# Sixteen 32x32 tiles for the query side, one stock of PSUM, and both FFN weights cast by their transfers

## The chip, the cores and the metric

The kernel runs on one core of a Trainium2 chip. Its engines are TensorE (PE; its weight loads are listed apart as PEld), VectorE (DVE), ScalarE (ACT), GpSimd (POOL) and SyncE (SP). Each works through its own instructions in their order and waits at semaphores for the others. Matmuls write only to PSUM, which has 8 banks of 512 fp32 per partition. Data come from and go to the main memory by DMA; a transfer is issued by SP, ACT or POOL, and one issued by POOL can change the type on the way.

The metric is the device time of one execution in microseconds (us). A profile shows one execution; its span goes from the first to the last instruction.

## The reference

Four batches, four heads, 1088 positions, head size 32. Keys and queries go through two sketches of size 8, and the product of the two gives 64 features; linear attention follows, and a feed-forward layer with SiLU on all 4352 tokens of 128 values:

```python
def phi(x):                                     # S1, S2: 8 x 32
    a = einsum('rd,bhsd->bhsr', S1, x)
    b = einsum('rd,bhsd->bhsr', S2, x)
    return einsum('bhsi,bhsj->bhsij', a, b).reshape(..., 64)
q_p, k_p = phi(q), phi(k)
kv  = einsum('bhsf,bhsd->bhfd', k_p, v)
z   = sum(k_p, axis=2)
num = einsum('bhsf,bhfd->bhsd', q_p, kv)
den = einsum('bhsf,bhf->bhs', q_p, z)[..., None] + 1e-06
x   = (num / den).transpose(0, 2, 1, 3).reshape(4352, 128)
h   = x @ w_in                                  # 128 x 2048
out = (h * sigmoid(h)) @ w_out                  # 2048 x 128
```

All inputs and the output are fp32.

## The kernel before

**Layout.** Positions are split as 32 rows of 34 (`NY`): K and Q of a batch are loaded so that a partition is a head (4) times one of 32 rows, and 34 positions of 32 values lie along it. DVE transposes blocks of 32x32, so after `kt` or `qt` a partition is a head times a value. w_in is 128 x 2048, cut in 16 (`NJ`) blocks of 128 columns.

**Order.** Nothing is scheduled by a planner at build time: the text `ORDER` lists the steps, each line of it is executed from left to right, and so each engine's program has its instructions in this order. A step that waits holds up everything behind it on its engine.

**Keys of a batch b.** `kt` transposes K (DVE), `pk` makes the sketches by matmuls in fp32 on tiles of 64 rows x 32 columns of the array, `tk` transposes them back, four `kp` multiply the two sketches (bf16), `kv` sums keys times values in 18 matmuls; `zs`, `zc`, `mm` and `mk` make the sum z and put it as third weight beside the query sketches in `WQ` (L308). `kw` or, for batch 0, `kw_act` masks KV and puts it in `KVw` with a second copy in the other half of the partitions.

**Queries.** `qt` transposes Q; `pq` (L346) makes both sketches and the denominator's weights by fp32 matmuls on four 64x64 tiles: two groups `g` of positions times two pairs `r` of heads; `tq` transposes back; `dn` is four DVE operations on the denominator; `qo` makes the 64 features (bf16); `pt` transposes them; `nm` (L388) multiplies by KV, again on four 64x64 tiles; `xc` copies the result to `xT`, the FFN's input, in bf16. Each batch goes through this in two parts (positions 0 to 8 and 8 to 17 of 17 pairs), batch 0 in three.

**FFN.** Tokens are cut in ten chunks (`CHUNKS`). For each, `f1` (L415) multiplies xT by two blocks of w_in (four for chunks of at most 256 tokens), `sl` is the SiLU on ACT (L428), `f2` (L431) adds up the products with w_out in one bank `o_ps`, with w_out as weights and g as moving data. `ot` (L442) transposes o_ps on DVE to rows of 32 and stores them with four transfers on SP in pieces of 128 bytes, eight where the chunk crosses a batch.

**PSUM.** `psH`: two pairs of banks for h (and for some calls of batch 0 marked H); `psP`: one pair for pk, pq and nm; `psO`: one bank for o_ps and the zero matmuls; `psA`: one bank for z, m and kv.

**Loads.** S1 and S2 come by ACT's queue, four times repeated over `T16`, and DVE transposes them (`weights`, L234). w_in is loaded in fp32 by SP in four parts, and ACT casts it with `wic` (L458), which also permutes the columns so that a block is contiguous. w_out is cast by its transfer, which POOL issues in `wo` (L250). `zeros` (L228) are matmuls on zeros between the first steps.

Of the kernel before, what the change touches and what calls it, by code (L numbers as in the profile page):

```python
# [26 lines left out]
f2 0 0, f1 0 3, sl 0 2, f2 0 1, pt 0 4 10, kt 1 0 34
sl 0 3, nm 0 4 10 H, f2 0 2, xc 0 4 10 A, f2 0 3, dn 0 10 17
f1 1 0, sl 1 0, ot 0, f1 1 3, sl 1 3, pk 1
qo 0 10 17, f1 1 1, tk 1, f1 1 6, kt 2 0 34, f2 1 0  # L30
sl 1 1, qt 1 0 34, lv 1, lv 2, f1 1 7, f2 1 1
sl 1 6, pt 0 10 17, f1 1 2, sl 1 7, sl 1 2, zs 1
pk 2, f1 1 5, zc 1 A, mm 1, tk 2, f1 1 4
sl 1 5, sl 1 4, f2 1 2, f2 1 3, nm 0 10 17 H, xc 0 10 17 A
mk 1, zs 2, kp 1 1 0, pq 1 0 8, kp 1 0 0, f1 2 3
f1 2 1, kp 1 0 1, f2 1 4, zc 2 A, f2 1 5, f2 1 6
sl 2 3, sl 2 1, f1 2 0, f2 1 7, sl 2 0, f1 2 5
tq 1 0 8, kp 1 1 1, sl 2 5, kv 1, f1 2 2, sl 2 2
dn 1 0 8, ot 1, f2 2 0, f1 2 4, sl 2 4, qo 1 0 8
kw 1, f2 2 1, f1 2 6, sl 2 6, f2 2 2, pt 1 0 8  # L40
kt 3 0 34, pq 1 8 17, nm 1 0 8 H, f1 2 7, f2 2 3, xc 1 0 8 A
sl 2 7, f2 2 4, f1 3 0, sl 3 0, tq 1 8 17, pk 3
f1 3 1, f2 2 5, lv 3, sl 3 1, dn 1 8 17, qo 1 8 17
pt 1 8 17, f1 3 5, mm 2, f2 2 6, tk 3, f1 3 7
mk 2, sl 3 5, sl 3 7, f2 2 7, f1 3 2, ot 2
nm 1 8 17, f1 3 3, f2 3 0, sl 3 2, f2 3 1, qt 2 0 34
sl 3 3, xc 1 8 17 V, f1 3 6, kp 2 1 1, f2 3 2, sl 3 6
f1 4 2, kp 2 0 0, pq 2 0 8, f1 4 3, tq 2 0 8, kp 2 1 0
sl 4 2, f2 3 3, sl 4 3, f1 3 4, pq 2 8 17, kp 2 0 1
sl 3 4, f1 4 7, sl 4 7, dn 2 0 8, kv 2, tq 2 8 17  # L50
f1 4 1, sl 4 1, f2 3 4, qo 2 0 8, kw 2, f1 4 0
f2 3 5, sl 4 0, f2 3 6, pt 2 0 8, f2 3 7, ot 3
f1 4 6, f1 4 4, nm 2 0 8, zs 3, f2 4 0, sl 4 6
sl 4 4, xc 2 0 8 V, dn 2 8 17, qt 3 0 34, f1 4 5, f2 4 1
f1 5 1, f2 4 2, qo 2 8 17, sl 4 5, zc 3 V, sl 5 1
f2 4 3, f1 5 0, sl 5 0, f2 4 4, kp 3 1 1, f1 5 5
f2 4 5, f2 4 6, f1 5 4, sl 5 5, sl 5 4, f2 4 7
pt 2 8 17, f1 5 7, mm 3, nm 2 8 17, kp 3 1 0, f1 5 3
sl 5 7, ot 4, mk 3, f2 5 0, f1 5 2, xc 2 8 17 V
sl 5 3, sl 5 2, pq 3 0 8, f1 5 6, sl 5 6, f2 5 1  # L60
tq 3 0 8, f1 6 1, sl 6 1, pq 3 8 17, f1 6 4, kp 3 0 0
f2 5 2, dn 3 0 8, sl 6 4, f1 6 2, f2 5 3, tq 3 8 17
qo 3 0 8, kp 3 0 1, f2 5 4, f1 6 0, sl 6 2, f2 5 5
f1 6 7, pt 3 0 8, kv 3, dn 3 8 17, sl 6 0, kw 3
sl 6 7, f1 6 5, f2 5 6, f2 5 7, f1 6 6, sl 6 5
nm 3 0 8, f1 6 3, ot 5, xc 3 0 8 V, sl 6 6, f2 6 0
f2 6 1, f1 7 4, sl 6 3, sl 7 4, f2 6 2, f1 7 5
f2 6 3, f2 6 4, sl 7 5, f1 7 1, f2 6 5, qo 3 8 17
f1 7 6, f2 6 6, sl 7 1, f1 7 0, f2 6 7, sl 7 6
sl 7 0, f1 7 2, pt 3 8 17, sl 7 2, nm 3 8 17, f1 7 3  # L70
ot 6, f2 7 0, f1 7 7, f2 7 1, xc 3 8 17 V, sl 7 3
sl 7 7, f1 8 1, f2 7 2, f1 8 5, f2 7 3, sl 8 1
f2 7 4, f1 8 2, f2 7 5, sl 8 5, f1 8 0, f2 7 6
f2 7 7, sl 8 2, f1 8 4, sl 8 0, f1 8 3, ot 7
# [15 lines left out]
def kernel(  # L90
# [22 lines left out]
    NH = NY // 2  # L113
# [94 lines left out]
    for i in range(2):  # L208
        nc.gpsimd.memset(KT[i][:, S:], 0.0)
# [300 lines left out]
```

## Time and profile before

Median of three runs 104.25 us (103.95 to 105.39).

| | us |
|---|---|
| profiled execution | 105.12 |
| its span | 103.1 |
| TensorE busy (864 matmuls) | 89.6 |
| ACT busy | 75.8 |
| DVE busy | 67.7 |
| POOL busy | 12.1 |
| mean granted TensorE clock | 0.949 |

Read the busy times as shares of stages: DVE works mostly in the first two thirds, TensorE and ACT from about 18 us to 97 us. Matmuls are pipelined, and the busy time of one contains its latency: a matmul of 128x512 shows as 379 ns, while two of them take 0.43 us in the chain. In the lists "x16" is the number of instructions; an fp32 matmul counts as two.

### The profile page before, as it was taken

The page shows a single profiled execution, that of the slowest core. Times are in us where ns is not written, and L with a number is a line of the kernel's source. Part 1 is how long each engine was busy: PE and PEld are TensorE (multiplying, and loading weights), DVE is VectorE, ACT ScalarE, POOL GpSimd, SP SyncE. Part 2 cuts the span into 40 slices and gives each one's busy share as a digit, 9 for nine tenths or more (in the row PEclk, how much of TensorE's full clock was granted, in tenths as well). Part 3 has the DMA queues.
Part 4 walks back from the last instruction along what each step waited for, and adds up shares of the span by engine and source line. Part 5 has one row for each costly group of instructions (what it writes and reads, how often), then busy time and mean ns, then how long its engine had stood idle before and what let it go on. Part 6 is the DMA issues. An engine that isn't in the chain of part 4 may idle for free.

```text
span 103.1 us, 2192 instructions
## 1 busy us (share of the span) xinstructions
PE 89.6 (87%) x864; PEld 47.1 (46%) x864; DVE 67.7 (66%) x130; ACT 75.8 (73%) x91; POOL 12.1 (12%) x48
## 2 busy tenths in 40 slices
PE   5719988909999999999999999999999999999700
PEld 5602876506535564443344444434544344456500
DVE  0072999794489999999999999689994230201200
ACT  0506619945297699799999779998988999997500
POOL 5608950002620000000000000000000000000000
PEclk9995999997699999999999999999999999999985
DMA  1898999999690004000400041140003141032331
GB/s 40 281 237 270 304 382 323 331 345 221 87 130 8 0 3 76 7 0 8 85 0 0 6 69 33 31 71 0 6 15 65 22 78 24 0 57 45 69 58 23
DMA packets 23214, 9.82 MB, mean 95 GB/s; under 512 B 19236, under 2 KB 21540, under 8 KB 23204
## 3 DMA queue, kind: packets, MB, share of 16 engines
q1 hardware_dynamic: 20768, 8.29, 30.5%
q0 software_dynamic: 2256, 1.36, 9.3%
q8 instruction: 7, 0.11, 0.5%
q10 hardware_dynamic: 180, 0.02, 0.1%
q14 instruction: 3, 0.02, 0.1%
HBM read 8.80 MB, written 2.23 MB: 107 GB/s over the span
## 4 chain that ended last, share of the span: by engine, by line
PE 63%; DMA 16%; DVE 9%; ACT 1%; POOL 1%; ACTq 1%; issue 1%; DVEq 0%; POOLq 0%
PE o_ps L439 28%; PE h_ps L421 25%; DMA w_out_bf<-in_moe_w_out_dram 13%; DMA T<-in_S_dram 3%; PE pq_ps L354 3%; PE num_ps L395 2%; ACT g L428 1%; DVE PQ L360 1%; DVE kp L286 1%; PE z_ps L295 1%; PE pk_ps L273 1%; DVE KT L260 1%; ACTq L178 1%; DVE o_tt L445 1%; DVE qp L380 1%; PE kv_ps L318 1%
## 5 line engine op out<-in xcount | busy, mean ns | idle before, releaser
L428 ACT ACTIVATE g<-h_ps 128x1024 bf16<-128x1024 f32 (+2 forms) x72 | 65.6, 979 | 10.6 <-PE h_ps L421 10.1
L439 PE MATMUL o_ps<-g,w_out_bf 128*128 128x512 bf16 (+4 forms) x160 | 38.7, 355 | 2.8 <-DMA w_out_bf<-in_moe_w_out_dram 2.6
L421 PE MATMUL h_ps<-xT,w_in_bf 128*128 128x512 bf16 (+4 forms) x160 | 40.8, 351 | 0.1
L439 PEld LDWEIGHTS <-w_out_bf 128*128 128x128 bf16 x160 | 15.5, 100 | 17.3 <-DMA w_out_bf<-in_moe_w_out_dram 2.9
L421 PEld LDWEIGHTS <-w_in_bf 128*128 128x128 bf16 x160 | 14.3, 99 | 16.9 <-issue 7.0
L445 DVE STREAM_TRANSPOSE o_tt<-o_ps 128x512 f32<-128x512 f32 (+4 forms) x10 | 6.3, 634 | 18.7 <-PE o_ps L439 18.6
L286 DVE TENSOR_TENSOR kp<-pk 128x576 bf16<-128x576 f32 x16 | 11.4, 740 | 0.0
L232 PE MATMUL zps<-zw 128*128 128x128 bf16 x112 | 9.6, 249 | 1.1 <-POOL hm L199 1.1
L380 DVE TENSOR_TENSOR qp<-PQ 128x1024 bf16<-128x1024 f32 (+4 forms) x9 | 10.3, 1142 | 0.1
L232 PEld LDWEIGHTS <-zw 128*128 128x128 bf16 x112 | 8.1, 115 | 3.5 <-issue 2.3
L158 POOL DMA_DIRECT2D Vb<-in_v_dram x12 | 6.5, 546 | 11.8 <-DMA w_out_bf<-in_moe_w_out_dram 9.1
L360 DVE STREAM_TRANSPOSE PQ<-pq_ps 128x512 f32<-128x512 f32 (+3 forms) x8 | 5.7, 714 | 1.7 <-PE pq_ps L354 1.6
L386 DVE STREAM_TRANSPOSE qT<-qp 128x512 f32<-128x512 f32 (+4 forms) x9 | 6.0, 671 | 0.2
L354 PE MATMUL pq_ps<-QT,WQ 64*64 64x256 f32 (+3 forms) x64 | 5.3, 401 | 0.1
L343 DVE STREAM_TRANSPOSE QT<-Qx 128x1088 f32<-128x1088 f32 (+2 forms) x5 | 5.3, 1056 | 0.0
L260 DVE STREAM_TRANSPOSE KT<-Kx 128x1088 f32<-128x1088 f32 (+2 forms) x5 | 5.2, 1049 | 0.0
L273 PE MATMUL h_ps<-KT,WK 64*32 64x288 f32 x16 | 2.4, 683 | 3.0 <-DVE KT L260 3.0
L236 DVE STREAM_TRANSPOSE ST<-T 32x32 f32<-32x32 f32 x4 | 0.8, 202 | 5.6 <-DMA T<-in_S_dram 5.6
L226 ACT ACTIVATE w_in_bf<-w_in_f 128x512 bf16<-128x512 f32 x4 | 4.3, 1122 | 0.1
L226 ACT ACTIVATE Vb<-Vx 128x576 bf16<-128x576 f32 x2 | 1.3, 674 | 3.7 <-DMA Vx<-in_v_dram 3.7
L218 ACT ACT_TABLE_LOAD x1 | 1.3, 1283 | 3.4 <-issue 3.4
L337 ACT ACTIVATE KVw<-kv_ps,hm 64x64 bf16<-64x64 f32 (+1 forms) x6 | 1.5, 306 | 3.0 <-PE kv_ps L318 3.0
(53 smaller groups left out, 52.5 us busy)
## 6 DMA issues: line engine op xcount, KB each, us to landing
Kx<-in_k_dram SPq DMA_DIRECT2D x3, 544.0 KB, 10.4
Qx<-in_q_dram SPq DMA_DIRECT2D x3, 544.0 KB, 14.8
w_in_f<-in_moe_w_in_dram SPq DMA_DIRECT2D x4, 256.0 KB, 4.8
out_dram<-o_tt SPq DMA_DIRECT2D x16, 64.0 KB, 1.9
Vb<-in_v_dram POOLq DMA_DIRECT2D x9, 72.0 KB, 14.6
w_out_bf<-in_moe_w_out_dram POOLq DMA_DIRECT2D x1, 512.0 KB, 13.5
out_dram<-o_tt SPq DMA_DIRECT2D x8, 56.0 KB, 1.8
Vx<-in_v_dram SPq DMA_DIRECT2D x3, 144.0 KB, 4.1
```

Source lines behind the costliest of these rows:

```text
L158: ins = eng.dma_start(dst, src)
L232: nc.tensor.matmul(t["zps"][:, :ncol], zw, zw[:, :ncol], start=True, stop=True)
L260: nc.vector.transpose(out=KT[b % 2][:, y0 * 32: y1 * 32], in_=Kx[b][:, y0:y1, :].rearrange("p a d -> p (a d)"))
L286: eng.tensor_tensor(out=o, in0=bcast(s[:, :, 0, 4 * e: 4 * e + 4], 2, R), in1=bcast(s[:, :, 1], 3, 4), op=ALU.mult)
L354: nc.tensor.matmul(t["pq_ps", b, p0][64 * g: 64 * (g + 1), r, :cols].rearrange("p (y x) -> p y x", x=32), w[rs, :], qv[rs, g, p0:p1, :], s ...
L360: nc.vector.transpose(out=PQ[b % 2][:, p0:p1].rearrange("p y r f -> p r y f"), in_=t["pq_ps", b, p0][:, :, :cols].rearrange("p r (y f) -> ...
L380: nc.vector.tensor_tensor(out=t["qp", b][:, p0:p1].rearrange("p y r j i -> p (y r) j i"), in0=bcast(fa, 2, R), in1=bcast(fb, 3, R), op=ALU ...
L386: nc.vector.transpose(out=dst.rearrange("p r (y x) -> p y r x", x=32), in_=src)
L421: nc.tensor.matmul(h[:, i, :], w_in_bf[:, j * P: (j + 1) * P], xT[:, t0: t0 + ntok], start=True, stop=True)
L428: nc.scalar.activation(out=gv, in_=t.pop(("h", c, s)), func=ACT.Silu)
L439: nc.tensor.matmul(op[c][:, :ntok], w_out_bf[:, j, :], g[:, i, :], start=(j == 0), stop=(j == NJ - 1))
L445: nc.vector.transpose(out=o_tt[:, :ntok], in_=op[c][:, :ntok])
```

## The change

**Query side.** A batch (batch 0: three parts) is one call. `pq` and `nm` work on sixteen tiles of 32x32: head `i` by group `c` of four positions, each row of tiles into a bank of its own, so that a call takes two pairs of banks. Blocks of positions are now quadruples, nine for 34 (`NQ`), and QT is padded. `tq` and `xc` come in two calls, one for each pair; `dn`, `qo` and `pt` handle the whole call.

**KV.** `km` masks KV by heads into (2, head, value) in bf16, on DVE, or on ACT in four activations; `kr` multiplies it by the 0/1 matrix `same`, which copies each 32-row strip to all four; `kw` copies the result to `KVw`.

**PSUM.** One stock `psX` of three pairs of banks. Each step names its pair (0, 1, 2) in ORDER: f1, pk, pq and nm share it. `psO` and `psA` stay.

**Weights.** w_in is cast by a transfer that POOL issues in `wi`, after the first part of K has landed; `wo` follows at once. K of batch 1 waits for w_in, Q of batch 1 for w_out. `wic` is gone, and f1 reads its weights with a step of four columns. S1 and S2 are loaded once, by SP and ACT, turned by four matmuls with a unit matrix (`turned`), and masked by one DVE operation.

**Last 768 tokens.** Their order within xT is another. In chunks 8 and 9, f2 takes g as weights and w_out as moving data, 128 columns at a time, so that o_ps holds tokens by row; `ot` copies it and stores it in pieces of 1 KB, two transfers for chunk 8 and one for chunk 9. Chunk 9's o_ps is a pair of the stock. The chunks' bounds from 3136 on are others.

**Order.** ORDER is written anew as a whole; its first lines and a middle part stand below.

```diff
-CHUNKS = [..., (3136, 512), (3648, 512), (4160, 192)]
+CHUNKS = [..., (3136, 448), (3584, 512), (4096, 256)]
+ROWS = 3584
 ORDER = """
-weights, vc0 0 2, kt 0 0 18, kt 0 18 34, zeros 33, pk 0 0 2 H
-weights2, zeros 3, pk 0 2 4, qt 0 0 8, tk 0, zeros 13
...
+wi, wo, zeros 14, turned, weights, kt 0 0 18
+weights2, kt 0 18 27, zeros 14, pk 0 0 0 2, kt 0 27 34, pk 0 -1 2 3
+wq_const, qt 0 0 8, zeros 1, pk 0 -1 3 4, tk 0, kp 0 0 0
+zeros 13, zs 0, zc 0 A, kp 0 1 0, zeros 8, mm 0
+vc0 0 2 A, mk 0 A, kp 0 0 1, vc0 2 4 A, kp 0 1 1, zeros 8
+pq 0 0 2 1 2, zeros 3, kv 0, tq 0 0 2 0, tq 0 0 2 1, dn 0 0 2
+same_const, km 0 A, qo 0 0 2, qt 0 8 34, zeros 18, kr 0
+pt 0 0 2, kw 0 V, zeros 10, pq 0 2 9 0 1, tq 0 2 9 0, zeros 11
+nm 0 0 2 2 0, xc 0 0 2 0 A, tq 0 2 9 1, dn 0 2 5, xc 0 0 2 1 A, zeros 12
+f1 0 0 1, qo 0 2 5, sl 0 0, pt 0 2 5, f1 0 1 2, zeros 12
+nm 0 2 5 0 1, kt 1 0 34, f2 0 0, sl 0 1, xc 0 2 5 1 A, xc 0 2 5 0 A
+dn 0 5 9, f1 0 3 2, qt 1 0 34, f1 0 2 1, sl 0 3, sl 0 2
+pk 1 0, qo 0 5 9, f1 1 3 2, f2 0 1, lv 1, sl 1 3
...
+f1 4 1 2, sl 4 1, f2 3 4, f1 4 0 1, f1 4 4 0, f2 3 5
+qo 2 0 9, kv 2, km 2 V, f1 4 2 2, sl 4 0, f1 4 6 1
+pt 2 0 9, sl 4 4, sl 4 2, kr 2, f1 4 3 0, f2 3 6
+f2 3 7, kw 2 V, sl 4 6, mm 3, ot 3, sl 4 3
+nm 2 0 9 2 1, xc 2 0 9 0 V, mk 3 V, xc 2 0 9 1 V, f2 4 0, f1 4 7 0
...
+f2 8 6, sl 9 1, f2 9 0 1, f2 8 7, sl 9 3, f2 9 1
+ot 8 V, f2 9 2, f2 9 3, ot 9 V
 """
...
+    def bank2(slot, name):
+        return psX.tile([P, 2, CH], FP32, name=f"{name}{slot}", tag=f"x{slot}")
...
+    def turned():
+        t["st"] = psA.tile([P, 2 * R], FP32, name="st_ps", tag="ac")
+        for i in range(4):
+            nc.tensor.matmul(t["st"][32 * i: 32 * (i + 1), :], T16, I16, start=True, stop=True,
+                             tile_position=(0, 32 * i))
...
+    def wi():
+        t["wi"] = begin(nc.gpsimd, w_in_bf, moe_w_in, k0a)
+        load_kq(nc.sync, 1, k, Kx, after=t["wi"])
+    def wo():
+        ins = begin(nc.gpsimd, w_out_bf.rearrange("p (i e) m -> p i (e m)", e=4), ...)
+        load_kq(nc.sync, 1, q, Qx, after=ins)
+        for b in range(2, B):
+            load_kq(nc.sync, b, k, Kx)
+            load_kq(nc.sync, b, q, Qx)
...
+    def kr(b):
+        t["kr", b] = psA.tile([P, 2, H, D], FP32, name="kr_ps", tag="ac")
+        nc.tensor.matmul(..., same, t["km", b].rearrange("p e h d -> p (e h d)"), ...)
+    def kw(b, copy):
+        copy(KVw[b], t["kr", b])
...
+    def pq(b, q0, q1, s0, s1):
+        t["pq", b, q0] = ps = [bank2(s0, "pq_ps"), bank2(s1, "pq_ps")]
+        for c in range(4):
+            for i in range(H):
+                rs = slice(32 * i, 32 * (i + 1))
+                nc.tensor.matmul(ps[i // 2][32 * c: 32 * (c + 1), i % 2, :cols]..., WQ[rs, b, i % 2, :],
+                                 qv[rs, c, q0:q1, :], ..., tile_position=(32 * i, 32 * c))
...
+    def nm(b, q0, q1, s0, s1):
+        t["nm", b, q0] = ps = [bank2(s0, "num_ps"), bank2(s1, "num_ps")]
+        for e in range(2):
+            for i in range(H):
+                for c in range(4):
+                    cs = slice(32 * c, 32 * (c + 1))
+                    nc.tensor.matmul(ps[c // 2][32 * i: 32 * (i + 1), c % 2, :cols],
+                                     KVw[b][cs, e, i, :], t["qT", b][cs, i, q0 * 32: q1 * 32, e],
+                                     ..., tile_position=(32 * c, 32 * i))
...
-            nc.tensor.matmul(h[:, i, :], w_in_bf[:, j * P: (j + 1) * P],
+            nc.tensor.matmul(h[:, i, :], w_in_bf[:, CH * (j // 4) + j % 4: CH * (j // 4 + 1): 4],
                              xT[:, t0: t0 + ntok], start=True, stop=True)
...
+            if t0 >= ROWS:                              # f2
+                if j == 0 and not two:
+                    nc.tensor.matmul(op[c][:, :ntok], zw, bcast(zw, 1, n), start=True, stop=False)
+                for h in range(n):
+                    nc.tensor.matmul(op[c][:, h * P: (h + 1) * P],
+                                     g[:, i, h * P: (h + 1) * P], w_out_bf[:, j, :], ...)
...
+        if t0 >= ROWS:                                  # ot
+            copy(o_tt[:, :ntok], op[c][:, :ntok])
+            for i in range(ntok // (2 * P)):
+                nc.sync.dma_start(dst, o_tt[:, 2 * P * i: 2 * P * (i + 1)])   # pieces of 1 KB
+            return
```

In ORDER, `pq b q0 q1 s0 s1` and `nm` name the two pairs they take, `f1 c s slot` and `pk b slot` one; A and V say whether ACT or DVE copies. The engine's order on DVE after the first slice is qt of the rest, pt, kw, tq; before it was pt, qt, xc.

381 lines of the change are left out of this document (186 added, 195 removed).

## Prediction

> **What bounds the kernel now.** I read in this order: the busy table in stretches over the whole span, which splits it into a start (0 to about 28 us), a middle in which TensorE hardly rests, and an end after 97.4; then the chain that ended last (o_ps and h_ps matmuls 53%, the transfer of w_out 13%); then the waits; then the order of time at both ends.
>
> Start. The same table for each microsecond from 20 to 29 (stretch, length, then busy time and count of PE, PEld, DVE, ACT, POOL, granted clock, DMA share, GB/s):
>
> ```profile
> 20.00:21.00 1.00, 0.58 (x7) 0.27 (x4) 0.96 (x2) 1.00 (x2) 0.00 (x0) 1.00 1.06 323
> 21.00:22.00 1.00, 0.00 (x0) 0.00 (x0) 1.00 (x3) 0.77 (x1) 0.00 (x0) 1.00 1.11 338
> 22.00:23.00 1.00, 0.00 (x0) 0.00 (x0) 1.00 (x2) 0.00 (x0) 0.00 (x0) 1.00 1.12 360
> ...
> 25.00:26.00 1.00, 1.00 (x12) 0.55 (x5) 0.00 (x0) 0.83 (x2) 0.07 (x1) 0.50 1.29 177
> 26.00:27.00 1.00, 1.00 (x7) 0.69 (x6) 0.00 (x0) 0.00 (x0) 0.47 (x1) 0.50 0.66 87
> ```
>
> From the waits (engine, line, releaser, us, times, longest):
>
> ```profile
> ACT g L428 <- PE h_ps L421: 10.1, 19, 2.5
> ...
> PE o_ps L439 <- DMA w_out_bf<-in_moe_w_out_dram: 2.6, 1, 2.6
> ```
>
> TensorE stands from 20.6 to 23.2 because w_out, issued at 9.6 behind POOL's other work, lands at 23.2. Just after that the clock is 0.5 for about 3.4 us (24.4 to 27.8), so matmuls take twice as long: another 1.7 us. The first SiLU of chunk 1 starts at 27.83.
>
> Middle and end, in order of time (start, us, engine, what):
>
> ```profile
> 87.45 0.59 PE L421 MATMUL h_ps<-xT,w_in_bf 128*128 128x512 bf16 x2
> ...
> 94.98 0.72 DVE L445 STREAM_TRANSPOSE o_tt<-o_ps 128x512 f32<-128x512 f32 x1 [5.31 <-PE o_ps L439]
> ...
> 95.75 1.67 PE L439 MATMUL o_ps<-g,w_out_bf 128*128 128x192 bf16 x16
> ...
> 97.46 0.38 DVE L445 STREAM_TRANSPOSE o_tt<-o_ps 128x192 f32<-128x192 f32 x1 [1.76 <-PE o_ps L439]
> ```
>
> In the middle, pairs of 512-column matmuls follow each other every 0.43 us in the chain, 0.421 ns per column. From 27.83 to the last matmul's end (97.43) are 69.6 us. The work in it: 130,304 columns of FFN matmuls (4352 x 32, less 8,960 done before) = 54.9 us; and for batches 1 to 3 keys 1.95, z 1.3, m 0.3, KV 1.6, six query calls 3.8, seven numerator calls 2.6. Together 66.4: TensorE is the bound, and only 3.2 us are lost, 0.8 of them where chunk 9's second FFN matmul waits for the bank of chunk 8 (94.98 to 95.75). ACT (10.1 us of waits) follows TensorE. After 97.43 come a transpose, four output issues, of which the third holds SP for 1.5 us (98.75), their landing and the close: 5.7 us to the span's end at 103.1.
>
> **The start.** (1) Weights. w_in and w_out are both cast to bf16 by their transfers, issued by POOL right after its memsets, and K of batch 1 waits for w_in, Q of batch 1 for w_out. w_in's issue waits for the first K piece (landing about 4.3: issued some 0.4 later than now, 2.9 us to land). Queued on POOL behind that wait are L4, WQ's constants and the new `same` matrix; with about 0.95 us per issue (the row of w_out) they start at 6.3 and need some 4 us by the nearest memsets and selects, while KV's mask is first needed about 12.5. The software queue moved 1.36 MB (bf16) in 9.3% of 16 engines x 103 us, or 7.2 us of all engines for both weights; K, Q and V of batch 0 are 1.67 MB, 5.1 us at 330 GB/s. From 2 us on, with K of batch 1 in between, w_out lands at 15 to 18. The first f2 asks for it at 20, so the 2.6 and the 1.7 us go. ACT loses four casts of 1.1 us, which lay in its waits.
>
> (2) Until the first f1. S1 and S2 lead their queues and are turned by TensorE (8 tiny matmuls) where DVE did four transposes after 5.59; keys' matmuls end near 8.0 instead of 10.2. From there DVE's line is as before (tk 0.78, four kp of 0.74), so the queries' first transpose comes 2 us earlier, at about 12. Then the change adds: two transposes for one (0.17), qt of the rest put ahead of pt (1.0), the KV copy behind the mask, matmul and pt (0.4), half of the next tq, which must free a bank pair that the numerator takes (0.65), and xT in two ACT copies (0.3); the 1.0 us by which qt held xT goes. Net, first f1 at 17.8 instead of 18.3.
>
> (3) From there to chunk 1: dn, qo, pt of the second slice (1.0, 0.95, 0.55) end at 19.7, numerator and first f2 at 20.2, two copies and the SiLUs (about 0.9 each back to back) follow on ACT, and the first SiLU of chunk 1 starts at 23.0 against 27.83: **-4.8 us**. If w_out is late all of it but the 0.5 goes.
>
> **The middle**, from that same point. FFN: 133,376 columns (three f2 of chunk 0 are still due), 56.2 us. Keys, z, m, KV as before: 5.1. Queries: one call of 32 instructions on 32x32 tiles per batch for two of 8 on 64x64. No row has sixteen tiles. The nearest, from TensorE's order of time:
>
> ```profile
> 14.85 1.67 PE L232 MATMUL zps<-zw 128*128 128x128 bf16 x27
> ...
> 31.73 0.71 PE L273 MATMUL pk_ps<-KT,WK 64*32 64x288 f32 x16
> 33.92 0.39 PE L395 MATMUL h_ps<-qT,KVw 64*64 64x224 bf16 x8
> ...
> 34.67 0.66 PE L354 MATMUL pq_ps<-QT,WQ 64*64 64x256 f32 x8
> ```
>
> 16 instructions on eight 64x32 tiles take about as long as 8 on four 64x64: the count of tiles hardly counts. Bounds: 0.65, and 2.6 if only four tiles run together. I take 0.7 (nearest: eight tiles), three times 2.1. Numerator: 8 instructions on 224 columns took 0.39, in the chain also at 288 columns; now 32; bounds 0.38 and 1.5, taken 0.5, with the last part of batch 0 1.95. Both at their upper ends would add 8.7 us. The copying matmul `same`: 0.2 each, 0.6. Sum of these 9.8. On DVE dn is one set of four instead of two (saves 0.5 a batch); qo, pt, tq, kw come out equal within 0.2. Its list from 19.7 to xT of batch 3 adds up to 53 us, so to 73 at the earliest; TensorE needs batch 3 only after chunk 6, about 75: just hidden, at nothing.
>
> Chunks 8 and 9 put g as weights and move w_out: 96 matmuls of 128 columns, each with its weight load. Nearest is the row of 27 zero matmuls of that shape (14.85, 1.67 us): 62 ns against 54 for 128 columns, +0.8, and 0.2 for one zeroing matmul. [...]
>
> w_in is now read as weights with a step of four elements, the permutation that ACT's cast used to do. No row shows a stepped weight load. [...] Moving data with a step of two (qT) costs nothing visible: 2 x 288 columns in 0.38. I take 0.
>
> Work 56.2 + 1.0 + 9.8 = 67.0. Losses: 3.2 less 0.8 (chunk 9 has its own bank pair), plus 1.0 I allow for the shared pairs. 70.4 from 23.0: last matmul at **93.4**, 0.8 us more than before for the stretch (+0.8).
>
> **The end.** Rows come out token by token: copy of 256 (0.4), one issue (0.45) instead of four, landing 1.9, close 0.8: 3.55 for 5.7, **-2.1**. Chunk 8's two issues go out ahead of it.
>
> Sum: -4.8 + 0.8 - 2.1 = -6.1: span 97.0. The profiled execution was 105.12 for a span of 103.1, 0.9 over the median 104.25 of the runs; from the median the forecast is 98.1.
>
> **The rivals.**
> *The shared stock stalls TensorE.* Queries and numerator each take two of three pairs, until DVE or ACT has emptied them: 0.7 + 2 x 0.78 and 0.5 + 1.4. Then one pair is left for h, and f1, latency and SiLU go in turn: 0.43 + 0.17 + 1.03 = 1.6 a slice against TensorE's 0.86. Six times some 1.3 slices: 6 us, of which I booked 1: 103. Against it: f2 of ten stored g can fill the gaps, and three pairs are one more than h has now outside those times.
> *w_out is late all the same*, both weights in one queue: at the 13.5 us that w_out took now for one, it lands at 23 or later, the wait and the slow clock return, 4.3 of the 4.8: 102.4. Against it: now five more Q and K loads were issued beside it.
> *Slower: stepped weight loads.* The place is f1, 160 loads. [...] For it: nothing in the trace shows such a load; against it only the stepped moving reads. [...]
>
> **How the numbers follow.** Forecast 0.67; stock 0.12 (103); late w_out 0.07 (102.4, so half and half); stepped loads 0.11, of which 0.03 mild (102) and 0.08 beyond 240 ns; tiles that run four at a time 0.03 (106.8). Two per cent is about what a measurement of this kernel can tell from no change: 102.2 and 106.3. Faster 0.67 + 0.03 + 0.03 = 0.73, within 0.16, slower 0.11. Range: below, no stalls added and both tiled calls at their floors, with losses of 1 us: 94.5; above, the stock's stalls and w_out's: 103.5. Outside are the 0.11 that are slower, some 0.05 of the stalls and 0.04 below.
>
> **What would show it.** w_out landing before 18 and no clock of 0.5 after 20; first SiLU of chunk 1 near 23.0; query calls of 0.7 and numerators of 0.5; w_in's loads near 99 ns; last matmul near 93.4 and 3.5 us behind it. Waits of f1 on SiLU or copies above 6 us in sum, or weight loads above 200 ns, make it wrong.

## The result and the profile after

The changed kernel takes 99.52 us (median of four runs, 99.29 to 100.22); the kernel before took 104.73 in the same series (103.95 to 105.39). The ratio is 0.952, with a 95% interval of 0.942 to 0.961: faster by almost 5%. The forecast was 98.1 with a range of 94.5 to 103.5. The profiled execution took 99.32 us with a span of 97.6.

The first stage again in a table of stretches, of the changed kernel (stretch, length, then busy time and count of PE, PEld, DVE, ACT, POOL, granted clock, DMA share, GB/s):

```profile
20.00:21.00 1.00, 0.50 (x35) 0.42 (x36) 1.00 (x2) 0.74 (x1) 0.00 (x0) 1.00 1.05 357
21.00:22.00 1.00, 0.73 (x8) 0.56 (x6) 0.97 (x3) 0.55 (x2) 0.00 (x0) 1.00 1.13 356
22.00:23.00 1.00, 1.00 (x21) 0.59 (x20) 0.70 (x3) 0.72 (x1) 0.00 (x0) 1.00 1.07 340
...
25.00:26.00 1.00, 1.00 (x10) 0.76 (x8) 1.00 (x2) 1.00 (x2) 0.00 (x0) 1.00 1.17 373
26.00:27.00 1.00, 1.00 (x40) 0.55 (x38) 1.00 (x3) 1.00 (x2) 0.00 (x0) 1.00 1.04 302
```

TensorE no longer stands from 20.6 to 23.2 (one pause of 0.27 us is left, below), and the granted clock at 25 to 27 is 1.00 where it was 0.50. The transfers' list says why (tile, queue, instructions, KB, us from issue to landing):

```profile
w_in_bf<-in_moe_w_in_dram POOLq DMA_DIRECT2D x1, 512.0 KB, 8.2
w_out_bf<-in_moe_w_out_dram POOLq DMA_DIRECT2D x1, 512.0 KB, 10.3
```

w_out was issued at 5.53 and landed at 15.9 instead of 23.2; TensorE does not wait for it now. From the changed kernel's waits (engine, line, releaser, us, times, longest):

```profile
ACT g L470 <- PE h_ps L463: 5.6, 8, 1.0
...
PE pq_ps L383 <- ACT WQ L229: 0.8, 1, 0.8
```

ACT waits 5.6 us for h instead of 10.1. The second line is new: the first query matmul waits for a third of its weights, because their copy stands on ACT behind a cast of V. The second part of V landed at 10.74 here (9.0 to 12.1 in the variants below), against 8.42 in before; both weights are under way beside it now.

TensorE of the changed kernel in order of time (start, us, engine, what):

```profile
18.17 1.03 PE L463 MATMUL h_ps<-xT,w_in_bf 128*128 128x256 bf16 x8
19.04 0.83 PE L238 MATMUL zps<-zw 128*128 128x128 bf16 x12
20.50 0.33 PE L425 MATMUL num_ps<-qT,KVw 32*32 32x96 bf16 x32 [0.63 <-DVE qT L416]
20.77 0.61 PE L493 MATMUL o_ps<-g,w_out_bf 128*128 128x256 bf16 x4
21.21 0.49 PE L463 MATMUL h_ps<-xT,w_in_bf 128*128 128x256 bf16 x3
21.97 0.71 PE L463 MATMUL h_ps<-xT,w_in_bf 128*128 128x256 bf16 x5 [0.27 <-issue]
```

First f1 at 18.17, first f2 at 20.77, and before the last five matmuls of chunk 0's f1 a pause for which the trace names no engine and no tile ("issue"; more on it in the last section). The first SiLU of chunk 1 follows at 24.1. At the other end:

```profile
90.35 2.84 PE L488 MATMUL o_ps<-w_out_bf,g 128*128 128x128 bf16 x48
91.89 0.69 DVE L226 COPY o_tt<-o_ps 128x512 f32<-128x512 f32 x1 [7.16 <-PE o_ps L488]
92.61 1.94 SPq L508 DMA_DIRECT2D out_dram<-o_tt  x3
93.23 0.42 DVE L226 COPY o_tt<-o_ps 128x256 f32<-128x256 f32 x1 [0.65 <-PE o_ps L488]
```

The last matmul ends at 93.2, the last copy at 93.65, and the three issues of SP (two of chunk 8, one of chunk 9) run one behind the other from 92.61 to 94.55.

So the span of 103.1 became 97.6. I divide it at the same two points as the prediction did, here for every profiled kernel that the experiments below add (us):

| kernel | first SiLU of chunk 1 | last matmul's end | between them | from there to the span's end |
|---|---|---|---|---|
| before | 27.83 | 97.4 | 69.6 | 5.7 |
| before, w_out first | 26.14 | 95.6 | 69.5 | 4.5 |
| before, w_out first, queries earlier | 24.57 | 94.2 | 69.6 | 4.5 |
| before, zeros while waiting | 28.16 | 97.7 | 69.5 | 4.5 |
| after | 24.1 | 93.2 | 69.1 | 4.4 |
| after, contiguous w_in blocks | 25.3 | 94.2 | 68.9 | 4.4 |
| after, old order of the last tokens | 24.1 | 92.6 | 68.5 | 6.0 |
| after, query matmuls twice | 23.8 | 96.0 | 72.2 | 4.4 |
| after, half of SiLU | 23.3 | 92.0 | 68.7 | 4.4 |
| after, one kp on POOL | 23.6 | 92.6 | 69.0 | 4.4 |
| after, loads not held | 25.1 | 94.2 | 69.1 | 4.5 |
| after, without zeros | 25.6 | 94.6 | 69.0 | 4.4 |
| after, last store on ACT | 26.3 | 95.4 | 69.1 | 4.2 |
| after, four edits together | 23.5 | 92.4 | 68.9 | 4.2 |

The third column stays between 68.5 and 69.6 except where query work is done twice, the last one between 4.2 and 4.5 except in two rows; the first one moves everywhere. Two things limit what can be read from it. Each row is one execution: up to its last store "last store on ACT" is the same program as "after", and its profiled execution, the longest of its six, reaches that SiLU 2.2 us later (V landed at 12.06 in it, and the clock was 0.5 from 11.65 to 18.48). So a difference in this column between two rows of the changed kernel does not by itself show an effect of the edit. And the point does not mark the same work in both kernels: there the kernel before has done all four f2 of chunk 0, the changed kernel two, so 0.9 us of TensorE's work has moved from its start to its middle.

### The profile page after: what moved, and what is told of

Same layout as the page of the kernel before. It is cut to its first block, busy times and chain, and to the rows that moved or that the text cites. A ratio compares the mean times of both kernels' runs of the same rounds, so it can differ in the third digit from the quotient of the medians.

```text
span 97.6 us, 2784 instructions
## 1 busy us (share of the span) xinstructions
PE 88.2 (90%) x1161; PEld 52.8 (54%) x1161; DVE 66.1 (68%) x106; ACT 71.8 (74%) x98; POOL 15.2 (16%) x57
## 4 chain that ended last, share of the span: by engine, by line
PE 45%; DMA 18%; ACT 13%; DVE 13%; POOL 4%; issue 3%; DVEq 0%; POOLq 0%
PE h_ps L463 19%; PE o_ps L493 15%; ACT g L470 12%; DMA w_out_bf<-in_moe_w_out_dram 11%; DMA Qx<-in_q_dram 7%; PE o_ps L488 6%; DVE kp L310 3%; PE num_ps L425 2%; DVE PQ L390 1%; DVE QT L373 1%; DVE KT L287 1%; DVE qp L410 1%; PE kv_ps L340 1%; DVE o_tt L510 1%; POOL Vb L219 1%
## 5 line engine op out<-in xcount | busy, mean ns | idle before, releaser
L463 PE MATMUL h_ps<-xT,w_in_bf 128*128 128x512 bf16 (+3 forms) x160 | 38.6, 348 | 0.4 <-issue 0.3
L493 PE MATMUL o_ps<-g,w_out_bf 128*128 128x512 bf16 (+3 forms) x128 | 31.8, 352 | 0.4 <-DVE o_tt L510 0.4
L493 PEld LDWEIGHTS <-w_out_bf 128*128 128x128 bf16 x128 | 12.1, 99 | 11.9 <-issue 1.7
L510 DVE STREAM_TRANSPOSE o_tt<-o_ps 128x512 f32<-128x512 f32 (+3 forms) x8 | 5.1, 633 | 10.1 <-PE o_ps L493 10.0
L410 DVE TENSOR_TENSOR qp<-PQ 128x2304 bf16<-128x2304 f32 (+3 forms) x6 | 10.5, 1744 | 0.1
L390 DVE STREAM_TRANSPOSE PQ<-pq_ps 128x576 f32<-128x576 f32 (+2 forms) x10 | 6.0, 638 | 1.3 <-PE pq_ps L383 1.2
L287 DVE STREAM_TRANSPOSE KT<-Kx 128x1088 f32<-128x1088 f32 (+3 forms) x6 | 5.5, 925 | 1.7 <-DMA Kx<-in_k_dram 1.7
L488 PE MATMUL o_ps<-w_out_bf,g 128*128 128x128 bf16 x96 | 6.0, 219 | 0.0
L488 PEld LDWEIGHTS <-g 128*128 128x128 bf16 x96 | 5.7, 98 | 0.3
L416 DVE STREAM_TRANSPOSE qT<-qp 128x1152 f32<-128x1152 f32 (+3 forms) x6 | 5.7, 956 | 0.1
L297 PE MATMUL pk_ps<-KT,WK 64*32 64x288 f32 x64 | 4.9, 482 | 0.4 <-DVE KT L287 0.4
## 6 DMA issues: line engine op xcount, KB each, us to landing
w_out_bf<-in_moe_w_out_dram POOLq DMA_DIRECT2D x1, 512.0 KB, 10.3
```

Source lines behind the costliest of these rows:

```text
L287: nc.vector.transpose(out=KT[b % 2][:, y0 * 32: y1 * 32], in_=Kx[b][:, y0:y1, :].rearrange("p a d -> p (a d)"))
L390: nc.vector.transpose(out=PQ[b % 2][:, q0:q1, 2 * u: 2 * u + 2].rearrange("p y r f -> p r y f"), in_=t["pq", b, q0][u][:, :, :cols].rearra ...
L410: nc.vector.tensor_tensor(out=t["qp", b][:, q0:q1].rearrange("p y h j i -> p (y h) j i"), in0=bcast(fa, 2, R), in1=bcast(fb, 3, R), op=ALU ...
L463: nc.tensor.matmul(h[:, i, :], w_in_bf[:, CH * (j // 4) + j % 4: CH * (j // 4 + 1): 4], xT[:, t0: t0 + ntok], start=True, stop=True)
L488: nc.tensor.matmul(op[c][:, h, :P] if two else op[c][:, h * P: (h + 1) * P], g[:, i, h * P: (h + 1) * P], w_out_bf[:, j, :], start=(j == 0 ...
L493: nc.tensor.matmul(op[c][:, :ntok], w_out_bf[:, j, :], g[:, i, :], start=(j == 0), stop=(j == NJ - 1))
```

## The experiments

The kernel before ran in each of four series (medians 104.73, 105.24, 104.73 and 105.17), the changed kernel in the first alone. Where a variant is set against its 99.52, the two stand in different series, and a difference of about half a us is within the scatter.

**Does the start alone explain it?** The kernel before, with nothing but w_out's load moved to the front of POOL's queue and the loads of batches 1 to 3 behind it:

```diff
-    for b in range(1, B): load_kq(..., k, Kx); load_kq(..., q, Qx)
 def wo():
-    begin(nc.gpsimd, w_out_bf..., moe_w_out..., v0)
+    ins = begin(nc.gpsimd, w_out_bf..., moe_w_out..., k0)      # behind the first part of K
+    load_kq(nc.sync, 1, k, Kx, after=ins)                      # then Q of 1, K and Q of 2 and 3
-weights, vc0 0 2, ...      ... f1 0 1, wo, sl 0 1
+wo, weights, vc0 0 2, ...  ... f1 0 1, sl 0 1
```

> The kernel before, with w_out issued first by POOL after the first K piece, and K and Q of batches 1 to 3 issued behind its landing. The prediction's theory (the late w_out costs 2.6 us of waiting and 1.7 us of half clock): first f2 no longer waits, no clock of 0.5 after 20 us, time 4.3 us under before, about 100.4. Rival (DVE or ACT is late next in the first third, so the wait is only covered): the wait goes but the first SiLU of chunk 1 comes less than 2 us earlier, time 102.5 or more.

Measured: 101.84 us (100.9 to 101.97), against 105.24 for before in the same series. The seven executions of before there are far apart (101.98 to 107.03), but all four of this kernel lie below them. By the medians 3.4 of some five us come with this one edit, between the two expectations and nearer to the rival's bound than to the theory's value. w_out was no longer waited for, but TensorE stood at another place. Order of time of this kernel:

```profile
18.84 0.56 PE L356 MATMUL pq_ps<-QT,WQ 64*64 64x192 f32 x8 [1.29 <-DVE QT L345]
19.33 1.51 PE L423 MATMUL h_ps<-xT,w_in_bf 128*128 128x256 bf16 x8
20.78 1.02 PE L356 MATMUL pq_ps<-QT,WQ 64*64 64x224 f32 x8
```

and its table of stretches:

```profile
19.00:20.00 1.00, 1.00 (x14) 0.61 (x10) 0.63 (x2) 0.00 (x0) 0.84 (x2) 0.88 1.13 369
20.00:21.00 1.00, 1.00 (x8) 0.53 (x10) 0.86 (x5) 0.97 (x2) 0.00 (x0) 0.50 1.08 371
...
22.00:23.00 1.00, 1.00 (x8) 0.75 (x6) 1.00 (x3) 0.00 (x0) 0.00 (x0) 0.50 1.14 372
```

The rest of batch 0's queries, now in competition with w_out, landed at 17.7. TensorE stood from 17.5 to 18.8, and then came 3.4 us at a clock of 0.5 (19.76 to 23.18): eight f1 matmuls in 1.51 instead of 1.05. One late load had been exchanged for another.

**The same with these queries two places earlier.**

```diff
 for i in range(4):
+    if i == 2: load_kq(nc.sync, 0, q, Qx, 8, NY)
     begin(nc.sync, w_in_f[:, i * CH:(i + 1) * CH], moe_w_in[:, i * CH:(i + 1) * CH])
-load_kq(nc.sync, 0, q, Qx, 8, NY)
```

> The kernel before with the w_out load first on POOL's queue, as in the earlier run of this kind (101.84 us), and in addition the second part of batch 0's queries issued ahead of the last two parts of w_in instead of behind them. There DVE waited 1.05 us for those queries at 17.75, TensorE stood 1.3 us and its clock fell to 0.5 for about 3.4 us. Theory (the start alone is the gain, and what was left of it in that run was this one late load): no wait for the queries, granted clock 1.00 between 16 and 28, first SiLU of chunk 1 between 24.2 and 25.0 instead of 26.14, 69.5 us from there to the last matmul, time 100.0 to 100.8. Rival (the new query side has a part in the gain): the clock holds, but the time stays at 101.4 or above.

Measured: 101.57 (100.61 to 101.83), before in that series 105.17; ratio 0.969, interval 0.962 to 0.976. The profiled execution, 100.61, does what the theory said. Its stretches (only the clock, the third number from the end, matters here) and the first SiLU of chunk 1:

```profile
16.00:20.00 4.00, 3.19 (x41) 1.94 (x40) 2.92 (x7) 3.56 (x8) 2.52 (x5) 1.00 1.22 280
20.00:24.00 4.00, 3.47 (x39) 2.57 (x36) 3.90 (x8) 3.94 (x5) 0.00 (x0) 1.00 1.09 362
24.00:28.00 4.00, 3.80 (x38) 1.63 (x39) 3.93 (x8) 3.43 (x5) 0.00 (x0) 1.00 1.12 339
```

```profile
24.57 4.33 ACT L431 ACTIVATE g<-h_ps 128x768 bf16<-128x768 f32 x6 [0.63 <-PE h_ps L424]
```

But it is the shortest of the four, and the median stays where the first version's was: by the time the rival's condition is met. With old query matmuls, old PSUM, four output issues and only another order of loads, the old kernel gets a span of 99.5 in the median, where before has 102.9 in this series and the changed kernel 97.8 in its own: two thirds of the gain. The remaining 1.7 us are not this order of loads. Of them the profiled executions show 0.5 in the first column of the table and 0.5 in the third; the rest lies in executions that were not traced. As 0.9 us of f2 have moved into the changed kernel's middle, that middle would be some 1.4 us shorter at equal work. No run has the changed kernel with the old query matmuls or the old PSUM, so what each part of the change brings to this last third was not separated.

**What the half clock costs.** The kernel before, with 44 zero matmuls to do while it waits for w_out:

```diff
-f2 0 0, f1 0 3, sl 0 2, ...
+zeros 44, f2 0 0, f1 0 3, sl 0 2, ...
```

> The kernel before with 44 zero matmuls more ahead of the first f2, so that TensorE is busy while it waits for w_out, which still lands at about 23.2. If the half clock after the wait costs 1.7 us by itself, the clock stays at 1.0 and the time falls by 1.0 to 1.7 us, to about 103.2. Rival (what follows is held by DVE and ACT, the clock costs nothing): within 0.4 us of before.

Measured: 103.95 (102.76 to 104.78) against 105.24: 1.3 us less by the medians, but inside the range of before in this series (101.98 to 107.03), so the times alone do not show it. In the profile the clock stayed at 1.00:

```profile
20.00:24.00 4.00, 2.85 (x48) 2.64 (x45) 3.90 (x8) 1.57 (x2) 0.00 (x0) 1.00 1.14 313
24.00:28.00 4.00, 2.95 (x31) 2.26 (x32) 0.36 (x2) 1.41 (x2) 2.29 (x5) 1.00 0.87 116
```

From the first f2 to the first SiLU of chunk 1 it is 3.1 us (25.05 to 28.16) instead of 4.6 (23.23 to 27.83). The half clock had cost 1.5 of the predicted 1.7. Here w_out landed at 25.0, 1.8 later than in the profile of before and than expected, which hides it in the span; no edit was made to that load, and why it was late is not shown. TensorE still stood 2.2 us here, after the zeros, and kept its clock; in before 2.6 us, and in the variant with w_out first 1.3, were followed by some 3.4 us at half. In these three the pause's length alone did not decide; the last section has what else the traces show.

**The same on the changed kernel, the other way round.** 63 zero matmuls taken out between 12 and 20 us:

```diff
-same_const, km 0 A, qo 0 0 2, qt 0 8 34, zeros 18, kr 0
+same_const, km 0 A, qo 0 0 2, qt 0 8 34, kr 0
...                                  # likewise zeros 10, 11, 12 and 12 in the next three lines
```

> The changed kernel without the 63 zeroing matmuls that its order has between the query part of batch 0's first tokens and the first matmul of the second FFN layer. They hold nothing up and nothing needs them. Theory (they fill the stretches in which TensorE waits for DVE, and keep the clock): TensorE stands for 1 us and more at a time from 13 to 20, the granted clock is 0.5 for one or two stretches of some 3.4 us between 14 and 25, first SiLU of chunk 1 at 25.1 to 25.8 instead of 24.1, time 100.5 to 101.3. Rival (the clock at the start has no price, since DVE and ACT set the pace there): within 0.4 of the changed kernel.

Measured: 100.34 (99.82 to 100.69), ratio to before 0.957 (0.950 to 0.964; the changed kernel has 0.952, 0.942 to 0.961). The stretches:

```profile
14.00:16.00 2.00, 0.37 (x15) 0.10 (x24) 1.97 (x4) 0.25 (x2) 0.52 (x2) 0.63 1.34 226
16.00:18.00 2.00, 1.28 (x64) 0.57 (x64) 1.38 (x4) 0.00 (x0) 1.90 (x5) 0.50 1.19 297
18.00:20.00 2.00, 1.36 (x36) 0.97 (x10) 1.83 (x6) 0.61 (x3) 0.32 (x1) 0.50 1.12 327
20.00:22.00 2.00, 1.56 (x39) 0.79 (x37) 1.97 (x3) 2.00 (x4) 0.00 (x0) 0.50 1.11 355
22.00:24.00 2.00, 2.00 (x11) 1.18 (x8) 1.90 (x6) 0.88 (x2) 0.00 (x0) 0.50 1.11 348
```

The clock is at 0.5 for some ten us, though TensorE is never without work for more than about 1.3 us in that time. The first SiLU of chunk 1 comes at 25.57, 1.5 later, as expected. The time is 0.8 above the changed kernel and 1.2 above the variant that ran beside it (99.1, below), a little under the expected values. The ranges overlap, so it is the profile that says it: the zero matmuls in ORDER, which the prediction did not mention for the changed kernel, are a part of its gain.

**Do the query matmuls and the shared PSUM set the middle?** Each query and numerator call of batches 1 to 3 done twice, with the same result:

```diff
-for c in range(4):                       # pq
+for c in [0, 1, 2, 3] * (2 if b else 1):
-for e in range(2):                       # nm
+for e in [0, 1] * (2 if b else 1):
```

> The changed kernel with every query and numerator matmul of batches 1 to 3 done twice into the same place: TensorE gets 3 x (0.7 + 0.5) = 3.6 us more, DVE and ACT the same. Theory (TensorE bounds the middle): time up by 3 us or more, to 102.5 or more, so the 0.8 us a batch that the sixteen tiles save count nearly in full. Rival (DVE and ACT, or the shared pairs, hold TensorE up and it has slack): up by less than 1.8.

Measured: 102.38 (101.65 to 102.88), ratio to before 0.976 (0.969 to 0.983). Order of time, once in the changed kernel and once here:

```profile
29.80 0.77 PE L383 MATMUL pq_ps<-QT,WQ 32*32 32x288 f32 x32
```

```profile
29.58 1.60 PE L383 MATMUL pq_ps<-QT,WQ 32*32 32x288 f32 x64
```

3.7 us of work were added to TensorE (0.83 and 0.39 a batch, three times), the time rose by 2.9 and the middle by 3.1. So over the middle as a whole TensorE is the bound, with about 0.6 us of slack, not DVE or ACT behind it.

**ACT relieved.** SiLU on the first half of each chunk's tokens only; the other half of g is zeros that POOL writes once at the start, so the results are other ones. Of the edit:

```diff
-nc.scalar.activation(out=gv, in_=t.pop(("h", c, s)), func=ACT.Silu)
+half = CHUNKS[c][1] // 2
+nc.scalar.activation(out=gv[:, :, :half], in_=t.pop(("h", c, s))[:, :, :half], func=ACT.Silu)
```

> The changed kernel with SiLU on the first half of each block's tokens only (the rest of g is zeros written once at the start by POOL): ACT loses some 28 of its 65 us, TensorE and DVE keep theirs. Theory (TensorE bounds, losses at the shared pairs are about 1 us): time down by at most 2 us, not under 97.5. Rival (ACT and the pairs it empties late set the middle): down by 3 us or more.

Measured: 98.31 (98.04 to 100.29), 1.2 less than the changed kernel. ACT now waits, from its waits:

```profile
ACT G L475 <- PE h_ps L466: 23.8, 46, 2.1
```

A SiLU takes 0.59 us instead of 1.02 (medians), so pairs of PSUM come free that much sooner, and yet the middle is only 0.3 shorter (68.7); the rest is at the start (23.3 instead of 24.1), ahead of what the edit can do. If the stock stalled TensorE as the prediction's first rival had it, most of its 5 us would have come back here.

**DVE relieved.** One of batch 1's key products moved to POOL (`kp 1 1 1 P`):

> The changed kernel with one of the four key products of batch 1 on POOL instead of DVE: DVE has 0.74 us less between 27 and 30 us, where the chain runs through it. If DVE is the bound of that stretch, queries of batch 1 come 0.7 us earlier and the time falls by 0.3 to 0.7. If TensorE is the bound there, no change within 0.2. If POOL is much slower than DVE at it, KV of batch 1 comes later and the time rises.

Measured: 98.82 (98.23 to 99.29), 0.7 less, as much as was expected if DVE were the bound; but the middle did not change (69.0), and the profile has its gain ahead of the edit: the pause before chunk 0's last f1 is missing in it, and the first SiLU of chunk 1 is at 23.6. On POOL the operation takes longer than DVE's 0.75:

```profile
25.81 1.18 POOL L310 TENSOR_TENSOR kp<-pk 128x576 bf16<-128x576 f32 x1 [13.37 <-DVE pk L304]
```

That DVE bounds 27 to 30 us is not shown by this.

**The stepped weight loads.** Blocks of w_in read contiguously. This leaves out the permutation, so hidden values meet other rows of w_out and the results are other ones:

```diff
-w_in_bf[:, CH * (j // 4) + j % 4: CH * (j // 4 + 1): 4]
+w_in_bf[:, j * P: (j + 1) * P]
```

> The changed kernel with w_in read as contiguous blocks of 128 columns instead of a step of four; hidden values then meet other rows of w_out, so this leaves out the permutation, with the same instructions and sizes. Theory (stepped weight loads cost nothing): loads near 99 ns instead of 114 and the time within 0.5 us of 99.5. Rival (the step costs, above all in chunks 0 and 9 where a matmul lasts 108 ns): 1 us or more faster.

Measured: 99.87 (98.96 to 100.92), no gain. The groups of the changed kernel and the loads' record in this one (ns min/median/max):

```profile
L463 PEld LDWEIGHTS <-w_in_bf 128*128 128x128 bf16 x160 | 17.1, 114 | 14.3 <-issue 3.8
L493 PEld LDWEIGHTS <-w_out_bf 128*128 128x128 bf16 x128 | 12.1, 99 | 11.9 <-issue 1.7
```

```profile
L463 PEld LDWEIGHTS <-w_in_bf x160: 95/98/99, 17.9 to 91.1; 128*128 128x128 bf16 x160
```

A step of four made a load 15 ns longer (medians 113 and 98), and the time shows nothing of it. This profile has a pause of 1.62 us at the place where the changed kernel's has 0.27:

```profile
23.19 0.71 PE L463 MATMUL h_ps<-xT,w_in_bf 128*128 128x256 bf16 x5 [1.62 <-issue]
```

**The last tokens.** Output of chunks 8 and 9 as of all others, through transposes and four issues each, with chunk 9 still in its own bank:

```diff
-ROWS = 3584
+ROWS = 1 << 20
-op[c] = (bank2(slot, "o_ps") if c == len(CHUNKS) - 1 ...
+op[c] = (bank2(slot, "o_ps")[:, 0, :] if c == len(CHUNKS) - 1 ...
```

> The changed kernel with the last 768 tokens done as all others: w_out as weights, o_ps transposed by DVE, stores of 128-byte pieces on four issues. Chunk 9 keeps a bank of its own. Theory: what follows the last matmul grows from 4.4 to about 5.7 us, f2 of chunks 8 and 9 gets 0.4 us shorter (56 against 54 ns, one zeroing matmul): time up by 0.9, to 100.4. By the prediction's figure (3.55 against 5.7, 62 ns): up by 1.1. Rival (the queue of output issues in front is what counts, and it is the same): within 0.3 of 99.5.

Measured: 99.97 (99.39 to 100.28), 0.45 more than the changed kernel, half of what was expected, and with overlapping ranges no difference that the times show. In the profile the end is 1.5 longer (6.0), since chunk 9's four issues stand behind chunk 8's four:

```profile
92.09 3.98 SPq L519 DMA_DIRECT2D out_dram<-o_tt  x8
```

The middle is 0.6 shorter (68.5), of which the 128-column matmuls (56 against 54 ns, 96 of them) and the zeroing (0.2) explain 0.4. Together that makes 1.0, near the 0.9 expected.

**The last store on another queue.** ACT has nothing left to do there:

```diff
-nc.sync.dma_start(dst, ...)
+(nc.scalar if c == len(CHUNKS) - 1 else nc.sync).dma_start(dst, ...)
```

> The changed kernel with the store of the last chunk issued on ScalarE's queue, which has nothing left to do, instead of as third on SyncE's. Theory: the last store starts at the end of its copy (93.65 in the profile of the changed kernel) instead of 0.35 us later, all else as it was: 0.3 us less, 99.0 to 99.3. Rival: the issue takes longer on that queue or its landing does, and the time is within 0.15 of the changed kernel.

Measured: 99.1 (97.83 to 101.35), ratio to before 0.944 (0.936 to 0.951). The median is as the theory has it, but the runs are 3.5 us apart, so that 0.3 cannot be told by them. In the profile the end is 0.2 shorter (4.2), and the landing is 2.2 us from ACT's queue as from SP's.

**The held loads.** K and Q of batch 1 issued without waiting for w_in and w_out:

```diff
-load_kq(nc.sync, 1, k, Kx, after=t["wi"])
+load_kq(nc.sync, 1, k, Kx)
-load_kq(nc.sync, 1, q, Qx, after=ins)
+load_kq(nc.sync, 1, q, Qx)
```

> The changed kernel with K and Q of batch 1 to 3 issued without waiting for w_in and w_out. Theory (the order of the loads is what brings w_out before its first use): w_out lands later than 15.9, at 20 or after, TensorE waits for it, time up by 0.5 to 3 us. Rival (two casts at the front are early enough without it): w_out lands before 20.5, Q of batch 1 a few us earlier, time unchanged or up to 0.3 us lower.

Measured: 99.99 (98.93 to 100.36), 0.5 more, at the lower end of what was expected and within the scatter, and by another way than either expectation had. The transfers' list:

```profile
w_out_bf<-in_moe_w_out_dram POOLq DMA_DIRECT2D x1, 512.0 KB, 16.2
```

16.2 us from issue to landing instead of 10.3: at 21.7, half a us ahead of the first f2 (22.17), which itself came later. What had moved was the start, with the first copy to xT at 19.08 instead of 17.67. The loads of batch 0 now share the engines with K and Q of batch 1: the second part of V landed at 11.60 instead of 10.74, the rest of the queries at 15.1 instead of 13.2. TensorE stood 2.63 us before the first query matmul, and the clock was 0.5 from 13.45 to 16.86. How much the loads and the clock each cost was not separated. In the changed kernel the chain that ended last runs through the held loads (w_out to 15.90, then the queries of batch 1 to 23.07) and DVE to 34.8; letting go of them gained nothing here.

**What the profile offered, put together.** The last store on ACT; the copy of the query weights ahead of the cast of V; the transpose of batch 1's queries behind that of its keys' sketches; one key product on POOL:

```diff
-vc0 0 2 A, mk 0 A, kp 0 0 1, vc0 2 4 A, ...
+mk 0 A, vc0 0 2 A, kp 0 0 1, vc0 2 4 A, ...
-dn 0 5 9, f1 0 3 2, qt 1 0 34, f1 0 2 1, ...   ... sl 1 0, tk 1, f1 1 6 2, ...
+dn 0 5 9, f1 0 3 2, f1 0 2 1, ...              ... sl 1 0, tk 1, qt 1 0 34, f1 1 6 2, ...
-sl 1 7, kp 1 1 1, ...
+sl 1 7, kp 1 1 1 P, ...
```

> The changed kernel with the last store on ScalarE's queue, and at the start: the copy that makes the last third of batch 0's query weights ahead of the first cast of V on ScalarE (the first query matmul waited 0.85 us for it), the transpose of batch 1's queries behind the transpose of its key projection on DVE (DVE waited 0.3 us for their load), and the first key product of batch 1 on POOL. Theory (what comes off the start comes off the end): first SiLU of chunk 1 at 23.2 to 23.6 instead of 24.1, 69.0 from there to the last matmul, 98.2 to 98.8. Rival (the query weights were waited for only because the queries were late as well): first SiLU of chunk 1 within 0.2 of the changed kernel, 98.9 to 99.3.

Measured: 98.09 (97.28 to 99.65), ratio to before 0.935 (0.928 to 0.941): clearly faster than before, and 1.0 below the variant with the last store alone, which ran beside it. The changed kernel did not run in this series; by the ratios to before, 0.935 (up to 0.941) against 0.952 (from 0.942), it is beaten too, just clear of the intervals. Its TensorE in order of time:

```profile
9.77 0.38 PE L383 MATMUL pq_ps<-QT,WQ 32*32 32x64 f32 x30
...
15.54 0.67 PE L383 MATMUL pq_ps<-QT,WQ 32*32 32x224 f32 x32 [1.73 <-DVE QT L373]
...
18.01 1.03 PE L463 MATMUL h_ps<-xT,w_in_bf 128*128 128x256 bf16 x8
```

The first query matmul no longer waits for its weights and starts 2 us earlier, but the next one then waits 1.73 us for the rest of the queries, so that f1 gains 0.16. In the profile the first SiLU of chunk 1 comes 0.6 earlier (0.27 of it is the "issue" pause, which this execution does not have), the middle and the end are 0.2 shorter each. Which of the four edits does most over all executions was not separated.

## Why the prediction was right, and where it was not

The mechanism was right: the gain is at the start, by weights that arrive in time and a clock that does not fall, and the middle is set by TensorE. Two thirds of the gain are shown by the old kernel with another order of loads; for the rest the cause is argued from the profiles. The sum was -6.1 us of span; it became -5.5, and that by three terms that were each mis-sized: start and end gave 1.9 less than forecast, the middle 1.3 more. That they nearly cancel is luck.

**The start, -4.8: measured -3.7.** w_out landed at 15.9, in the 15 to 18 of the prediction, and the wait (2.6) and the half clock (1.7; 1.5 by the zeros put into before) are gone. First f1 came at 18.17 instead of 17.8: the queries' weights waited 0.85 behind a cast of V, a queue on ACT that step (2) did not look at, and V itself came 2.3 later than in before. First f2 at 20.77 instead of 20.2. From there to chunk 1 it took 3.3 us instead of 2.8, with the "issue" pause in it. Against it stands that two thirds of the gain can be had in the old kernel by the order of loads alone, so what step (2) counted for the query side was small, as it said.

**The middle, +0.8: measured -0.5.** Query calls 0.75 to 0.82 (0.70 taken), numerators 0.49 (0.50), both near the row of eight tiles and far from their upper bounds. Token-major matmuls: 96 at 56 ns, from this line of the chain in the changed kernel (start, us, what):

```profile
90.51 2.69 PE o_ps L488 x48
```

The prediction took 62 ns from the zero matmuls, so 0.6 too much. One f2 more than reckoned was done at the starting point (0.4). Work of about 66.1 instead of 67.0, then, and 3.0 us of losses instead of 3.4. The 0.8 that the prediction took off for chunk 9's bank was misread: in before TensorE ran f1 of chunk 9 there until 95.60 and stood 0.15 us. So the losses are about those of before (3.2), and of the 1.0 allowed for the shared pairs the trace shows one wait: 0.25 us at 70.7, for a SiLU to empty a pair.

**The end, -2.1: measured -1.3, and nothing of it lasting.** The profile of before had one output issue of 1.5 us. Three variants with the old end, without such an issue, need 4.5 us from the last matmul to the span's end; the changed kernel needs 4.4. The step that failed is the comparison with one execution's 5.7. In the new end's own sum the copy (0.46 for 0.4) and issue and landing together (2.1 for 2.35) were near; the last issue starts 0.35 late behind chunk 8's two, though the text had them "ahead of it" for nothing, and the close took 1.5 instead of 0.8.

**The rivals.** *The shared stock* hardly stalled TensorE: 0.25 us in the trace, and half of SiLU's work brought 0.3 in the middle, not the 5 us of the rival. *w_out late* did not occur. Without the hold it landed at 21.7, later than the 20.8 at which the changed kernel asks for it, and was not waited for only because batch 0 was later too. *Stepped weight loads*: 114 ns against 98, far under the 200 that the prediction named as a sign. No run shows what a load of 200 ns or more costs, so the 0.11 with its 102 and 240 ns has no measured source; what the runs show is a load 15 ns longer without a time that tells (99.52 with the step, 99.87 without), and 48 matmuls that follow each other every 56 ns with a load of 98 ns each (above). *Four tiles at a time*: 0.77 for 32 instructions instead of 2.6, refuted. The range's lower end comes to 95.1 by its own terms, not 94.5.

**From the span to the time.** The prediction subtracted the profiled execution's 0.9 over the median. In the changed kernel it lies 0.2 under. Time outside the span is about 1.7 us in the runs of the changed kernel and its variants (1.65 to 1.86), and 1.9 to 2.1 in 21 of 25 later runs of before; 0.3 of the gain is thus in no trace, and its cause stays open.

## What to carry to other kernels

Split a span at events that both kernels have, and see which part moves; here one column of the table held most of the effect, two thirds of which the old kernel also got from a mere change in the order of loads. A load that arrived late cost its wait (2.6 us in before) and 1.5 us more through the clock here, so after moving one transfer forward, look for the next one that it has pushed back (here the queries in the old kernel, V in the changed one), and fill TensorE's gaps with zero matmuls (without 63 of them the changed kernel took 0.8 us more by the medians). Do not book a saving against an odd instruction of a single profile (an issue of 1.5 us among others of 0.4) without a second execution that shows it.

## What the runs showed of the hardware that was not expected

- While TensorE had work, the stretches at half clock in these traces lasted about 3.41 us or twice or three times that: 7.35 to 10.76 and 24.42 to 27.83 in before, 19.76 to 23.18 with w_out first, 8.7 to 12.15 with w_out first and queries earlier, 13.45 to 16.86 with the loads not held, 11.65 to 18.48 (6.83) with the last store on ACT, 14.5 to 24.75 (10.25) without zeros. A pause's length does not tell them: half clock came with pauses of 2.65 us (before), 2.63 (loads not held), 3.25 (last store on ACT) and 1.29 (w_out first, with smaller gaps), but not with 2.20 (zeros while waiting), 1.73 (four edits together) and 1.62 (contiguous blocks). TensorE's busy share in 3.41 us, and the granted clock right behind them:

  | kernel | stretch (us) | TensorE busy in it | clock behind it |
  |---|---|---|---|
  | before | 3.94 to 7.35 | 15% | 0.5 |
  | before | 21.00 to 24.42 | 35% | 0.5 |
  | after, without zeros | 11.09 to 14.50 | 41% | 0.5 |
  | before, w_out first | 16.35 to 19.76 | 52% | 0.5 |
  | after | 19.34 to 22.76 | 74% | 1.0 |
  | after | 9.10 to 12.52 | 75% | 1.0 |
  | before | 17.59 to 21.00 | 84% | 1.0 |

  Within a slow stretch, 3.41 us with TensorE busy for 40% and 68% (14.50 to 17.91 and 17.91 to 21.33 without zeros) and for 56% (11.65 to 15.06 with the last store on ACT) had more half clock behind them, 96% and 100% (7.35 to 10.76 and 24.42 to 27.83 in before) had not. What in general lowers the clock, and at which share, is not shown: no run was made to test it. The share of slow stretches in executions that were not traced stays open: their mean clock also counts the time after the last matmul, where it fell as well in before (at 99.51, 2.1 us after the last matmul's end).
- TensorE paused at about 21.5 us by 0.27 us in the changed kernel, by 1.62 us with contiguous blocks and not at all with half of SiLU. The trace names no engine for it, but the DMA records have loads of instructions (queue q8 of the page, 16 KB each). In the changed kernel the second of them ended at 20.47, and the matmul behind the pause began at 21.97, 1.50 us later. In before, such a load ran from 98.38 to 99.83, beside the odd issue of 1.5 us; the variant with w_out first and queries earlier, without an odd issue, has none there. That both are waits for the program itself is only argued; no run shows it.
- In the changed kernel, 32 fp32 instructions of 288 columns on sixteen 32x32 tiles took 0.77 us, hardly more than 16 on eight tiles (0.71).
- A weight load with a step of four bf16 columns took 113 ns (median, changed kernel), a contiguous one 98 (contiguous blocks).
